# ScalarE's order in a fused attention and two-layer kernel fixed by hand: exponentials issued apart from the scores, a decode step of VectorE placed earlier, the second pair's parts split by VectorE

## The chip, the cores and the metric

The program runs on one NeuronCore of a Trainium2 chip. Five engines work side by side, each through its own list of instructions in order: TensorE (PE, matmuls and transposes; PEld is its weight loads), VectorE (DVE), ScalarE (ACT), GpSimd (POOL) and SyncE (SP), which here only issues DMA transfers. They wait for each other through semaphores. The metric is the device time of one execution in microseconds (us), the median of several.

## What is computed

Causal attention with a memory term for 4 batches and 8 heads of 576 rows and 64 columns, then two feed-forward layers on the result. Cut to what matters:

```python
scores = scale * np.matmul(q, k.transpose(0, 1, 3, 2))      # causal mask, minus the row maximum
a = np.exp(scores); a /= a.sum(-1, keepdims=True) + 1e-09
local = np.matmul(a, v)
q_p = phi(q)                       # phi(x) = x + 1 for x > 0, else exp(x)
mem_out = np.einsum('bhsd,bhde->bhse', q_p, M_prev) / (np.einsum('bhsd,bhd->bhs', q_p, z_prev)[..., None] + 1e-06)
x = g * mem_out + (1 - g) * local  # g = sigmoid(beta), one number per head
x = softplus(x @ w_in) @ w_out     # 2304 x 512, inner width 2048
return (x @ w_a * (x @ w_b)) @ w_2 # inner width 1536
```

## The kernel before, in words

Work is float32, made of products of rounded parts: a number x is split into a high part (`qh`, `kh`, `gg`, `w`) and the rest (`ql`, `kl`), and three matmuls stand for one.

The attention works on 16 units, a unit being two heads of one batch. `attention()` is a software pipeline over them: in round n (n = 0 to 16) the unit `cur` = n makes its scores for rows 256 to 575 (`score(2)`, `score(3)`, `score(4)`), `prev` = n-1 has its exponentials transposed by TensorE (`turn`, `turn_tail`, the tiles `pe`), multiplied with v (`use`, the tile `po`) and finished, and `nxt` = n+1 has its parts made (`prep_k`: `kh`, `qh`, `kl`, `ql`; `prep_v`, `prep_v2`: `pos`, `neg`, `ph`, which is phi of q) and its first two score blocks done. `score(i)` is matmuls into `ps`, an instruction of VectorE that masks, scales and takes the row minimum (`mn`), and an exponential on ScalarE (`e`; `eT` for the last 64 rows of both heads). `memory` is the memory term (`pm` in PSUM, `mo` in SBUF), `turn_memory` transposes it into `mt`, `spread` transposes the reciprocal row sums into `pr`; ScalarE copies both out (`mt`, `rb`). `turn(A, ...)` has its PSUM tile copied out by ScalarE, `turn(V, ...)` by VectorE (both into `aT`). `finish` multiplies and adds (`xx`, by VectorE and then GpSimd), and SyncE stores `xx`.

The tiles `pe`, `pm`, `mt` and `pr` share one PSUM pool, `psT`, of two banks: a transpose into a new tile waits until the tile two before it has been copied out. In each round the order on TensorE ends with `mt`, a score block, `pr`, and ten short matmuls (`pt`); the next round begins with the transposes of head 0 (copied by ScalarE, called "first `aT`" below) and head 1 (copied by VectorE), a score block, and then two more groups of four transposes that take over those two banks.

Beside the attention `beside()` brings in the first weights of the feed-forward layers: a load (`wraw`), two VectorE instructions and a ScalarE one (lines 115, 118, 120), two and one more (122, 123 and the rounding copy `w`), one VectorE subtraction. Each `yield` of `attention()` runs one such step; rounds 1 to 16 have two yields each.

The order on PE, DVE and SP within the attention is that of the code (`manual_schedule`); ScalarE's and GpSimd's is chosen by the scheduler when the program is built, from a model of its own. The bank that a tile of a pool gets is chosen then too.

Of the kernel before, what the change touches and what calls it, by code (L numbers as in the profile page):

```python
# [10 lines left out]
AF = mybir.ActivationFunctionType  # L11
ALU = mybir.AluOpType
# [3 lines left out]
NP = H // 2  # L16
# [22 lines left out]
def tile_kernel(ctx: ExitStack, tc: tile.TileContext, qt, kt, vt, mp, zp, be, w_in, w_out, w_a, w_b, w_2, out):  # L39
    nc = tc.nc  # L40
    V, A, G, PE, SP = nc.vector, nc.scalar, nc.gpsimd, nc.tensor, nc.sync

    def f(ap):
        return ap.bitcast(F32)

    def rnd(eng, o, i):

        if eng is A:
            A.activation(out=o, in_=i, func=AF.Copy)  # L49
        elif eng is V:  # L50
            V.tensor_copy(out=o, in_=i)
        else:
            G.tensor_scalar(out=o, in0=i, scalar1=1.0, scalar2=0.0, op0=ALU.mult, op1=ALU.add)

    def sub(eng, o, a, b):
        eng.tensor_tensor(out=o, in0=a, in1=b, op=ALU.subtract)  # L56
# [22 lines left out]
    for j in range(2):  # L79
        G.affine_select(  # L80
            out=mask2[64 * j : 64 * j + 64, 1, 224:], in_=mask2[64 * j : 64 * j + 64, 1, 224:], compare_op=ALU.is_ge, fill=MASKED,
# [7 lines left out]
    gp = cst.tile([128, NP], F32, name="gp")  # L89
# [5 lines left out]
    def gates():  # L95
        A.activation(out=gt, in_=bt, func=AF.Exp, scale=-1.0)
        G.tensor_scalar(out=gt, in0=gt, scalar1=1.0, scalar2=1.0, op0=ALU.mult, op1=ALU.add)
        V.reciprocal(out=gt, in_=gt)
        pairs = gt.rearrange("p (n j) -> p n j", j=2)
        for j, r in enumerate(both):  # L100
            rnd(G, gp[r], pairs[r, :, j])
        G.tensor_scalar(out=og, in0=gt, scalar1=-1.0, scalar2=1.0, op0=ALU.mult, op1=ALU.add)
# [3 lines left out]
    later = mybir.DependencyInfo(mybir.DependencyClass.NoSync, mybir.DependencyReason.SCHED_ONLY)  # L106
# [47 lines left out]
    def load_m(b):  # L154
        m = mzs[b % 2]
        for j, r in enumerate((top, low)):
            SP.dma_start(out=m[r, :, 64 * j : 64 * j + 64], in_=mp[b, r])
            SP.dma_start(out=m[r, :, 128 + j], in_=zp[b, r])
        return G.tensor_tensor(out=m[:, :, 0:128], in0=m[:, :, 0:128], in1=gp.unsqueeze(2).to_broadcast([128, NP, 128]), op=ALU.mult)

    def heads(t, n, w=64):

# [2 lines left out]
    class Unit:  # L165
# [16 lines left out]
            SP.dma_start(out=vr[:, 0:4], in_=vt[b, p, 0:512].rearrange("(c p) e -> p c e", p=128))  # L182
            SP.dma_start(out=vr[0:64, 4], in_=vt[b, p, 512:576])

        def prep_k(self, first=False, after=None, hold=None):
            kr, qr = self.kr, self.qr
            part = lambda n, w: ap_.tile([128, w], F32R, tag=n, name=n, bufs=2)
            self.qh, self.ql, self.kh, self.kl = part("qh", 640), part("ql", 640), part("kh", S), part("kl", S)
            e = V if first else G
            if hold is None:  # L190
                rnd(e, self.kh, kr)
            else:
                i0 = G.tensor_scalar(out=self.kh, in0=kr, scalar1=1.0, scalar2=0.0, op0=ALU.mult, op1=ALU.add)
                tc.add_manual_dep(i0.ins, hold.ins.name, later, reason="order")
            i1 = A.activation(out=self.qh, in_=qr, func=AF.Copy)
            if after is not None:
                tc.add_manual_dep(i1.ins, after.ins.name, later, reason="order")
            sub(e, self.kl, kr, f(self.kh))
            sub(e, self.ql, qr, f(self.qh))

# [14 lines left out]
        def score(self, i):  # L215

            if i == 0:
                self.sm, self.mn, self.E = self.small("sm"), self.small("mn"), {}
            qh, ql, kh, kl, sm, mn, Es = self.qh, self.ql, self.kh, self.kl, self.sm, self.mn, self.E

            terms = ((qh, kh), (qh, kl), (ql, kh))
            ps = psS.tile([128, 2, 512], F32, tag="b", name="ps")
            if i < 4:
                L = 128 * (i + 1)
                qc = slice(128 * i, 128 * i + 128)
                for t, (a, b) in enumerate(terms):
                    for j, r in enumerate(both):
                        PE.matmul(out=ps[:, j, :L], lhsT=a[r, qc], rhs=b[r, 0:L], start=t == 0, stop=t == 2)  # L228
                wide = i > 1
                for j in range(2):  # L230
                    n = 2 * i + j
                    e = ap_.tile([128, 512 if wide else 256], F32, tag=f"e{wide}", name="e", bufs=8)[:, :L]
                    V.tensor_tensor_reduce(  # L233
                        out=e, in0=ps[:, j, :L], in1=mask1[:, 512 - L :], scale=-0.125, scalar=BIG, op0=ALU.add, op1=ALU.min,
                        accum_out=mn[:, n : n + 1],
                    )
                    A.activation(out=e, in_=e, func=AF.Exp, scale=-1.0, bias=mn[:, n : n + 1], accum_out=sm[:, n : n + 1])  # L237
                    Es[i, j] = e
                return
            e = ap_.tile([128, S], F32, tag="eT", name="eT", bufs=2)  # L240
            for c in range(2):
                cs = slice(288 * c, 288 * c + 288)
                for t, (a, b) in enumerate(terms):
                    PE.matmul(out=ps[:, c, :288], lhsT=a[:, 512:640], rhs=b[:, cs], start=t == 0, stop=t == 2)  # L244
            V.tensor_tensor_reduce(
                out=e.rearrange("p (c n) -> p c n", c=2), in0=ps[:, :, :288], in1=mask2, scale=-0.125, scalar=BIG,
                op0=ALU.add, op1=ALU.min, accum_out=mn[:, 8:9],
            )
            A.activation(out=e, in_=e, func=AF.Exp, scale=-1.0, bias=mn[:, 8:9], accum_out=sm[:, 8:9])
            Es["t"] = e  # L250

        def memory(self):

# [174 lines left out]
    order = [Unit(b, p) for b in range(B) for p in range(NP)]  # L428

    def attention():  # L430

        nu = len(order)
        order[0].loads_k()
        A.dma_start(out=bt, in_=be.partition_broadcast(128))
        order[1].loads_k()
        order[0].loads_v()
        order[0].prep_k(True)
        order[0].score(0)
        gates()
        order[0].score(1)  # L440
        first = load_m(0)
        order[0].prep_v()
        order[0].prep_v2()
        for n in range(nu + 1):
            cur = order[n] if n < nu else None
            prev = order[n - 1] if n else None
            nxt = order[n + 1] if n + 1 < nu else None
            i1 = None
            if prev:
                i1 = prev.turn(A, [(0, 0)])  # L450
                prev.turn(V, [(1, 0)])
            if nxt:
                nxt.prep_k(after=i1, hold=None if n else first)
            if cur:
                cur.score(2)
            if prev:
                prev.turn(A, [(0, 1), (0, 3)])
                prev.turn(V, [(1, 1), (1, 3)])
            if cur:
                cur.score(3)  # L460
            if prev:
                prev.over()
            if cur:
                cur.score(4)
                cur.sums()
            if prev:
                prev.turn(A, [(0, 2), (1, 2)])
                prev.turn_tail()
            if n + 2 < nu:
                order[n + 2].loads_k()  # L470
            if nxt:
                nxt.loads_v()
                if nxt.p == 0:
                    load_m(nxt.b)
                nxt.prep_v()
                nxt.score(0)
            if cur:
                cur.memory()
            if prev:
                prev.use()  # L480
                prev.turn_memory()
                yield n
            if nxt:
                nxt.score(1)
                nxt.prep_v2()
            if prev:
                yield n
                prev.spread()
                prev.finish()


# [24 lines left out]
                yield  # L516

    steps = beside()
    with tc.manual_schedule(engines={PE.engine, V.engine, SP.engine}):
        for n in attention():  # L520
            next(steps, None)
        for _ in steps:
            pass
# [21 lines left out]
    for gi, subs in enumerate(groups):  # L545
        xbs, ys, pend = [], [], []
        for b0, nb in subs:
# [3 lines left out]
            else:  # L551
                t = [psY2.tile([128, 2, TB], F32, tag=f"z{i}", name=f"z{i}") for i in range(KT // 2)]
# [131 lines left out]
```

## Time and profile before

| | |
|---|---|
| time, median of 3 runs | 1083.64 us (1083.64 to 1083.74) |
| the profiled execution: time, span | 1083.99 us, 1082.1 us |
| busy share of the span: PE, DVE, ACT, POOL | 97%, 44%, 41%, 15% |
| mean granted clock of TensorE | 0.996 of full speed |
| attention | about the first 240 us of the span |

The span is from the first to the last instruction of the profiled execution; what lies around it is 1.9 us. The profiled execution stands 0.35 us above the median of the runs. A busy share is a mean over stages with different limits: the feed-forward layers, after 240 us, have TensorE busy nearly throughout, and the attention is where engines wait for each other.

### The profile page before, as it was taken

The page shows a single profiled execution, that of the slowest core. Times are in us where ns is not written, and L with a number is a line of the kernel's source. Part 1 is how long each engine was busy: PE and PEld are TensorE (multiplying, and loading weights), DVE is VectorE, ACT ScalarE, POOL GpSimd, SP SyncE. Part 2 cuts the span into 40 slices and gives each one's busy share as a digit, 9 for nine tenths or more (in the row PEclk, how much of TensorE's full clock was granted, in tenths as well). Part 3 has the DMA queues.
Part 4 walks back from the last instruction along what each step waited for, and adds up shares of the span by engine and source line. Part 5 has one row for each costly group of instructions (what it writes and reads, how often), then busy time and mean ns, then how long its engine had stood idle before and what let it go on. Part 6 is the DMA issues. An engine that isn't in the chain of part 4 may idle for free.

```text
span 1082.1 us, 14889 instructions
## 1 busy us (share of the span) xinstructions
PE 1054.9 (97%) x5832; PEld 863.4 (80%) x5832; DVE 477.8 (44%) x1043; ACT 448.1 (41%) x924; POOL 165.9 (15%) x178
## 2 busy tenths in 40 slices
PE   5999999999999999999999999999999999999998
PEld 4776666678888988888888888888888888888897
DVE  4778787776776211111156679742122111111121
ACT  6888877764555322232244554432112111211121
POOL 7777776521000000000000000000000000000000
PEclk9999999999999999999999999999999999999999
DMA  5143425213434200010033354421000000100010
GB/s 170 57 135 104 151 91 157 85 61 110 155 117 156 89 10 1 36 43 1 1 98 98 117 175 141 152 78 59 1 0 20 20 1 1 39 1 1 1 39 21
DMA packets 45974, 75.43 MB, mean 70 GB/s; under 512 B 9552, under 2 KB 28496, under 8 KB 45904
## 3 DMA queue, kind: packets, MB, share of 16 engines
q1 hardware_dynamic: 45616, 74.15, 21.3%
q8 instruction: 46, 0.75, 0.3%
q10 hardware_dynamic: 288, 0.33, 0.1%
q14 instruction: 24, 0.20, 0.1%
HBM read 60.31 MB, written 14.16 MB: 69 GB/s over the span
## 4 chain that ended last, share of the span: by engine, by line
PE 89%; ACT 3%; POOL 2%; DMA 2%; issue 1%; DVE 1%; SPq 0%; ACTq 0%; DVEq 0%; POOLq 0%
PE pp L142 27%; PE ph L142 18%; PE y L142 16%; PE o L142 14%; PE ps L228 2%; PE pe L299 2%; PE po L341 2%; PE z L142 2%; PE pm L262 1%; PE ps L244 1%; ACT e L237 1%; DMA qr<-qt 1%; POOL neg L56 1%; PE pe L321 1%; PE mt L350 1%
## 5 line engine op out<-in xcount | busy, mean ns | idle before, releaser
L142 PE MATMUL pp<-xb,w 128*128 128x512 f32 (+1 forms) x1440 | 305.5, 368 | 0.0
L142 PEld LDWEIGHTS pp<-xb,w 128*128 128x128 f32 x1440 | 252.5, 188 | 46.0
L142 PE MATMUL ph<-xb,w 128*128 128x512 f32 (+1 forms) x960 | 210.5, 369 | 0.0
L142 PEld LDWEIGHTS ph<-xb,w 128*128 128x128 f32 x960 | 168.1, 189 | 30.4 <-issue 0.2
L142 PE MATMUL y<-gg,w 128*128 128x512 f32 x768 | 184.3, 389 | 0.0
L142 PEld LDWEIGHTS y<-gg,w 128*128 128x128 f32 x768 | 143.9, 188 | 29.8
L621 DVE TENSOR_TENSOR u<-pp,u 128x512 f32<-128x512 f32 (+1 forms) x60 | 38.3, 638 | 271.2 <-PE pp L142 271.2
L142 PE MATMUL o<-w,gg 128*128 128x512 f32 x648 | 157.0, 390 | 0.0
L142 PEld LDWEIGHTS o<-w,gg 128*128 128x128 f32 x648 | 120.8, 188 | 24.5
L56 DVE TENSOR_TENSOR gg<-s,gg 128x512 fp32r<-128x512 f32 (+1 forms) x80 | 51.0, 637 | 176.7 <-ACT gg L49 176.5
L390 ACT ACTIVATE s<-ph 128x512 f32<-128x512 f32 (+1 forms) x80 | 44.3, 554 | 165.5 <-PE ph L142 165.4
L620 ACT ACTIVATE u<-pp 128x512 f32<-128x512 f32 (+1 forms) x60 | 33.3, 556 | 176.4 <-PE pp L142 176.3
L49 ACT ACTIVATE gg<-u 128x512 fp32r<-128x512 f32 (+1 forms) x60 | 35.2, 587 | 120.4 <-DVE u L621 120.4
L237 ACT ACTIVATE e<-e,mn 128x128 f32<-128x128 f32 (+3 forms) x128 | 70.6, 555 | 4.0 <-DVE mn L233 3.9
L233 DVE CUSTOM_DVE_ANT_0 e<-ps,mask 128x128 f32<-128x128 f32 (+3 forms) x128 | 57.6, 487 | 22.1 <-PE ps L228 18.8
L120 ACT ACTIVATE wraw<-wraw 128x512 f32<-128x512 f32 x68 | 44.9, 674 | 37.0 <-DVE wraw L118 35.4
L299 PE MATMUL pe<-ident,e 128*128 128x128 f32 x320 | 47.7, 288 | 12.3 <-ACT mt L352 8.1
L49 ACT ACTIVATE w<-wraw 128x512 fp32r<-128x512 f32 x68 | 44.7, 671 | 31.9 <-DVE wraw L123 31.9
L56 DVE TENSOR_TENSOR w<-wraw,w 128x512 fp32r<-128x512 f32 x68 | 48.0, 718 | 15.9 <-ACT w L49 15.5
L299 PEld LDWEIGHTS pe<-ident,e 128*128 128x128 f32 x320 | 36.6, 145 | 21.2 <-ACT mt L352 9.6
L56 DVE TENSOR_TENSOR gg<-u,gg 128x512 fp32r<-128x512 f32 (+1 forms) x60 | 38.3, 638 | 32.2 <-ACT gg L49 32.2
L123 DVE SCALAR_TENSOR_TENSOR wraw<-wraw 128x512 uint32<-128x512 uint32 x68 | 49.3, 737 | 1.4
(97 smaller groups left out, 1038.2 us busy)
## 6 DMA issues: line engine op xcount, KB each, us to landing
wraw<-w_in SPq DMA_DIRECT2D x16, 512.0 KB, 3.6
wraw<-w_out SPq DMA_DIRECT2D x16, 512.0 KB, 4.7
wraw<-w_a SPq DMA_DIRECT2D x12, 512.0 KB, 3.7
wraw<-w_b SPq DMA_DIRECT2D x12, 512.0 KB, 3.6
wraw<-w SPq DMA_DIRECT2D x12, 512.0 KB, 3.6
qr<-qt SPq DMA_DIRECT2D x15, 320.0 KB, 3.5
kr<-kt SPq DMA_DIRECT2D x16, 288.0 KB, 3.2
xraw<-xs SPq DMA_DIRECT2D x9, 512.0 KB, 3.9
```

The lines of the kernel that those rows point to most:

```text
L49: A.activation(out=o, in_=i, func=AF.Copy)
L56: eng.tensor_tensor(out=o, in0=a, in1=b, op=ALU.subtract)
L120: A.activation(out=f(high), in_=f(high), func=AF.Identity, scale=REBIAS)
L123: V.scalar_tensor_tensor(out=high, in0=high, scalar=3, in1=low, op0=ALU.logical_shift_left, op1=ALU.bitwise_or)
L142: mm[0] = PE.matmul(out=o, lhsT=w(a), rhs=x(b), start=start and n == 0, stop=stop and n == 2, **kw)
L228: PE.matmul(out=ps[:, j, :L], lhsT=a[r, qc], rhs=b[r, 0:L], start=t == 0, stop=t == 2)
L233: V.tensor_tensor_reduce(out=e, in0=ps[:, j, :L], in1=mask1[:, 512 - L :], scale=-0.125, scalar=BIG, op0=ALU.add, op1=ALU.min, accum_out=m ...
L237: A.activation(out=e, in_=e, func=AF.Exp, scale=-1.0, bias=mn[:, n : n + 1], accum_out=sm[:, n : n + 1])
L299: PE.transpose(out=ps[:, 128 * n : 128 * n + 128], in_=Es[i, j][:, 128 * k : 128 * k + 128], identity=ident)
L390: A.activation(out=s, in_=ph, func=AF.Softplus)
L620: A.activation(out=u, in_=pab[0], func=AF.Copy)
L621: V.tensor_tensor(out=u, in0=pab[1], in1=u, op=ALU.mult)
```

## The change

- `attention()` now runs with ScalarE's order fixed too (`A.engine` in the set of `manual_schedule`). The exponentials are no longer issued in `score`, but by a method `exps`, at places of their own: those of score blocks 0 and 1, which the scheduler had spread, stand after `rb` and after the first `aT`, and that of `eT` stands directly behind `rb`.
- `neg` of the next unit (the exponential of phi) stands behind `rb` instead of ahead of `mt`.
- The first of the two yields in a round stands after `turn_tail`, so that its VectorE instructions run before the evacuation of score block 0, where they had run after `mo`.
- The second unit's `kh`, `kl`, `ql` are made by VectorE (`prep_k(True)` in round 0), where GpSimd made them.
- `gates()` comes behind the first two exponentials; the two artificial dependencies (`after`, `hold`) are gone.

```diff
-        def prep_k(self, first=False, after=None, hold=None):
+        def prep_k(self, first=False):
...
-            if hold is None:
-                rnd(e, self.kh, kr)
-            else:
-                i0 = G.tensor_scalar(out=self.kh, in0=kr, scalar1=1.0, scalar2=0.0, op0=ALU.mult, op1=ALU.add)
-                tc.add_manual_dep(i0.ins, hold.ins.name, later, reason="order")
-            i1 = A.activation(out=self.qh, in_=qr, func=AF.Copy)
-            if after is not None:
-                tc.add_manual_dep(i1.ins, after.ins.name, later, reason="order")
+            rnd(e, self.kh, kr)
+            rnd(A, self.qh, qr)
...
-                    A.activation(out=e, in_=e, func=AF.Exp, scale=-1.0, bias=mn[:, n : n + 1], accum_out=sm[:, n : n + 1])
...
-            A.activation(out=e, in_=e, func=AF.Exp, scale=-1.0, bias=mn[:, 8:9], accum_out=sm[:, 8:9])
...
+        def exps(self, *keys):
+
+            for k in keys:
+                e, n = self.E[k], 8 if k == "t" else 2 * k[0] + k[1]
+                A.activation(out=e, in_=e, func=AF.Exp, scale=-1.0, bias=self.mn[:, n : n + 1], accum_out=self.sm[:, n : n + 1])
...
+        order[0].prep_v()
         order[0].score(0)
+        order[0].exps((0, 0), (0, 1))
         gates()
         order[0].score(1)
-        first = load_m(0)
-        order[0].prep_v()
         order[0].prep_v2()
+        load_m(0)
...
-            if nxt:
-                nxt.prep_k(after=i1, hold=None if n else first)
+            if nxt and n:
+                nxt.prep_k()
             if cur:
+                cur.exps((1, 0))
                 cur.score(2)
...
             if cur:
+                cur.exps((1, 1))
                 cur.score(3)
+            if n == 0:
+                nxt.prep_k(True)
...
             if prev:
                 prev.turn(A, [(0, 2), (1, 2)])
                 prev.turn_tail()
+            if cur:
+                cur.exps((2, 0), (2, 1))
+            if prev:
+                yield n
...
-                nxt.prep_v()
                 nxt.score(0)
             if cur:
+                cur.exps((3, 0), (3, 1))
                 cur.memory()
+            if nxt:
+                nxt.prep_v()
             if prev:
                 prev.use()
                 prev.turn_memory()
+            if nxt:
+                nxt.score(1)
+            if prev:
+                prev.spread()
+            if cur:
+                cur.exps("t")
+                cur.sums()
+            if prev:
                 yield n
             if nxt:
-                nxt.score(1)
+                nxt.exps((0, 0), (0, 1))
                 nxt.prep_v2()
             if prev:
-                yield n
-                prev.spread()
                 prev.finish()
...
-    with tc.manual_schedule(engines={PE.engine, V.engine, SP.engine}):
+    with tc.manual_schedule(engines={PE.engine, V.engine, A.engine, SP.engine}):
```

How this moves instructions is shown at three places. The first is ScalarE around the end of a round; this is a round of before, from the copy `rt` to the `qh` of the round after it (no decode step happens to stand in it).

```order
L335 ACTIVATE rt<-pt 128x192
L237 ACTIVATE e,sm<-e,mn 128x128 x2
L209 ACTIVATE neg<-neg 128x640
L352 ACTIVATE mt<-mt 128x512
L359 ACTIVATE rb<-pr 128x512
L237 ACTIVATE e,sm<-e,mn 128x256 x2
L305 ACTIVATE aT<-pe,og 128x512
L195 ACTIVATE qh<-qr 128x640
```

The same engine with the change, round 1, between the same two instructions; L120 is a decode step that stands there in some rounds.

```order
L333 ACTIVATE rt<-pt 128x192
L248 ACTIVATE e,sm<-e,mn 128x384 x2
L248 ACTIVATE e,sm<-e,mn 128x512 x2
L199 ACTIVATE pos<-qr 128x640
L350 ACTIVATE mt<-mt 128x512
L357 ACTIVATE rb<-pr 128x512
L248 ACTIVATE eT,sm<-eT,mn 128x576
L120 ACTIVATE wraw<-wraw 128x512
L248 ACTIVATE e,sm<-e,mn 128x128 x2
L203 ACTIVATE neg<-neg 128x640
L303 ACTIVATE aT<-pe,og 128x512
L49 ACTIVATE qh<-qr 128x640
```

`mt` and `rb` have `pos` and the exponentials of blocks 2 and 3 ahead of them where `neg` stood, and between `rb` and the first `aT` there are now `eT`, two exponentials of 128 columns and `neg` (and in some rounds a decode step), where two of 256 columns stood.

The second place is TensorE in a middle round, before: the second four-transpose groups of `prev` and the waits that they carry.

```order
L228 MATMUL ps<-kh,ql 128x384 x2
L299 MATMUL pe<-ident,e 128x128 [waits Activation_49]
L299 MATMUL pe<-ident,e 128x128 x3
L299 MATMUL pe<-ident,e 128x128 [waits DVE_49]
L299 MATMUL pe<-ident,e 128x128 x3
L228 MATMUL ps<-kh,qh 128x512 x2
```

The same place with the change.

```order
L222 MATMUL ps<-kh,ql 128x384 x2
L297 MATMUL pe<-ident,e 128x128 [waits DVE_49]
L297 MATMUL pe<-ident,e 128x128 x3
L297 MATMUL pe<-ident,e 128x128 [waits Activation_49]
L297 MATMUL pe<-ident,e 128x128 x3
L222 MATMUL ps<-kh,qh 128x512 x2
```

TensorE's order is the same, but the two groups have exchanged banks: the first now waits for VectorE's `aT` and the second for ScalarE's. This is so in 13 of the 14 rounds from 2 to 15; round 8 is as before.

The third place is ScalarE at the end of the attention, the last round but one, before.

```order
L352 ACTIVATE mt<-mt 128x512
L359 ACTIVATE rb<-pr 128x512
L120 ACTIVATE wraw<-wraw 128x512
L390 ACTIVATE s<-ph_3512 128x512
L305 ACTIVATE aT<-pe,og 128x512
```

With the change (`s` is the softplus of the first feed-forward layer, which has another function table than the exponential).

```order
L350 ACTIVATE mt<-mt 128x512
L357 ACTIVATE rb<-pr 128x512
L248 ACT_TABLE_LOAD
L248 ACTIVATE eT,sm<-eT,mn 128x576
L120 ACTIVATE wraw<-wraw 128x512
L388 ACT_TABLE_LOAD
L388 ACTIVATE s<-ph_3512 128x512
L303 ACTIVATE aT<-pe,og 128x512
```

The last unit's `eT` now stands behind the first two softplus instructions, and two more table loads stand around it. On the other engines: VectorE has the three instructions of the second unit's parts and the moved decode steps; GpSimd makes `ph` after `xx` and `neg` ahead of `ss`; on SP the loads of the first decode step and two loads of `xraw` come ahead of the `kr` and `qr` loads that they had followed.

## Rows read from the trace of the kernel before

**Rows 1.** Busy time by stretch: length, then PE, PEld, DVE, ACT, POOL, clock, DMA.

```profile
26.00:240.00 214.00, 203.11 (x1721) 147.80 (x1718) 165.86 (x487) 166.54 (x432) 140.88 (x143) 0.98 0.34 105
```

**Rows 2.** Waits, 0 to 280 us: total, how often, the longest.

```profile
PE pe L299 <- ACT mt L352: 8.1, 9, 1.7
```

**Rows 3.** Timeline of PE: start, length, instruction, idle before it and its releaser.

```profile
34.16 0.66 PE L358 MATMUL pr<-ident,R 128*128 128x128 f32 x4
...
47.03 0.66 PE L358 MATMUL pr<-ident,R 128*128 128x128 f32 x4
...
160.88 1.15 PE L299 MATMUL pe<-ident,e 128*128 128x128 f32 x8 [1.66 <-ACT mt L352]
...
217.14 0.66 PE L358 MATMUL pr<-ident,R 128*128 128x128 f32 x4
...
220.35 1.09 PE L299 MATMUL pe<-ident,e 128*128 128x128 f32 x8
```

**Rows 4.** Groups of ACT, 26 to 240 us: count, busy, mean ns, idle before.

```profile
L305 ACT ACTIVATE aT<-pe,og 128x512 f32<-128x512 f32 x30 | 20.4, 680 | 1.9 <-PE pe L299 1.3
...
L249 ACT ACTIVATE eT<-eT,mn 128x576 f32<-128x576 f32 x15 | 11.5, 769 | 0.0
L237 ACT ACTIVATE e<-e,mn 128x128 f32<-128x128 f32 x28 | 10.9, 392 | 0.0
L209 ACT ACTIVATE neg<-neg 128x640 f32<-128x640 f32 x13 | 9.6, 737 | 24.0 <-POOL neg L56 24.0
...
L120 ACT ACTIVATE wraw<-wraw 128x512 f32<-128x512 f32 x10 | 6.8, 681 | 0.7 <-DVE wraw L118 0.7
...
L390 ACT ACTIVATE s<-ph 128x512 f32<-128x512 f32 x3 | 1.8, 599 | 5.8 <-PE ph L142 5.8
```

**Rows 5.** Timeline of ACT after `pr` in round 14.

```profile
217.89 0.60 ACT L359 ACTIVATE rb<-pr 128x512 f32<-128x512 f32 x1 [0.50 <-PE pr L358]
218.39 0.49 ACT L237 ACTIVATE e<-e,mn 128x256 f32<-128x256 f32 x1
```

**Rows 6.** Timelines of DVE and POOL: a decode instruction beside GpSimd and alone.

```profile
171.74 1.69 DVE L122 TENSOR_SCALAR wraw<-wraw 128x512 f32<-128x512 f32 x1
...
171.60 1.54 POOL L56 TENSOR_TENSOR neg<-qr,pos 128x640 f32<-128x640 f32 x1
...
217.94 0.43 DVE L122 TENSOR_SCALAR wraw<-wraw 128x512 f32<-128x512 f32 x1
```

**Rows 7.** Timelines of PE and DVE in the first 26 us.

```profile
17.18 0.47 PE L228 MATMUL ps<-kl,qh 64*128 64x128 f32 x2 [2.39 <-POOL kl L56]
...
24.94 0.66 PE L299 MATMUL pe<-ident,e 128*128 128x128 f32 x4 [0.59 <-ACT aT L305]
...
6.48 0.82 DVE L56 TENSOR_TENSOR ql<-qr,qh 128x640 fp32r<-128x640 f32 x1
...
12.11 0.69 DVE L233 CUSTOM_DVE_ANT_0 e<-ps,mask 128x512 f32<-128x512 f32 x1
```

**Rows 8.** Timelines of ACT and PE at the end of the attention.

```profile
226.39 1.28 ACT L390 ACT_TABLE_LOAD   x1
227.69 0.60 ACT L390 ACTIVATE s<-ph 128x512 f32<-128x512 f32 x1
...
236.31 0.59 ACT L359 ACTIVATE rb<-pr 128x512 f32<-128x512 f32 x1
...
239.20 0.68 ACT L305 ACTIVATE aT<-pe,og 128x512 f32<-128x512 f32 x1
...
239.94 1.45 PE L299 MATMUL pe<-ident,e 128*128 128x128 f32 x8 [0.39 <-ACT aT L305]
...
242.93 0.66 PE L321 MATMUL pe<-ident,eT 128*128 128x128 f32 x4 [0.66 <-DVE aT L307]
```

**Rows 9.** Busy time by stretch, columns as in rows 1.

```profile
116.00:122.00 6.00, 4.70 (x52) 3.35 (x48) 4.50 (x12) 5.18 (x11) 5.39 (x6) 1.00 0.02 5
160.00:166.00 6.00, 5.12 (x28) 3.79 (x28) 3.86 (x9) 5.69 (x14) 4.98 (x5) 0.72 0.12 37
```

More of the change, by code (lines that the diff above doesn't have):

```diff
@@ L158, in load_m @@
             SP.dma_start(out=m[r, :, 128 + j], in_=zp[b, r])
-        return G.tensor_tensor(out=m[:, :, 0:128], in0=m[:, :, 0:128], in1=gp.unsqueeze(2).to_broadcast([128, NP, 128]), op=ALU.mult)
+        G.tensor_tensor(out=m[:, :, 0:128], in0=m[:, :, 0:128], in1=gp.unsqueeze(2).to_broadcast([128, NP, 128]), op=ALU.mult)
     def heads(t, n, w=64):
@@ L447, in attention @@
             nxt = order[n + 1] if n + 1 < nu else None
-            i1 = None
             if prev:
-                i1 = prev.turn(A, [(0, 0)])
+                prev.turn(A, [(0, 0)])
                 prev.turn(V, [(1, 0)])
-            if nxt:
-                nxt.prep_k(after=i1, hold=None if n else first)
+            if nxt and n:
+                nxt.prep_k()
             if cur:
+                cur.exps((1, 0))
                 cur.score(2)
@@ L464, in attention @@
                 cur.score(4)
-                cur.sums()
             if prev:
```

## The prediction

> **What bounds the kernel now.** I read the busy time by stretch first, to see which engine has the least slack in the stage that the change touches. From 26 to 240 us TensorE is busy 203 of 214 us, VectorE 166, ScalarE 167, GpSimd 141 [rows 1]. TensorE is the bound, and whatever this change does must come through the 11 us in which it waits there, or through its granted clock (0.98 in the mean).
>
> The waits come next. The largest one that the change can reach is TensorE's second four-transpose groups waiting for ScalarE's copy `mt`: 8.1 us in nine places, 1.7 the longest [rows 2]. Why is that copy late? In ScalarE's groups `neg` has 24.0 us of idle time ahead of it, all ended by GpSimd's subtraction, in 13 rounds [rows 4]. ScalarE runs in order, and `mt` and `rb` stand behind `neg`. So the chain is: GpSimd late, ScalarE held at `neg`, the bank of `mt` not free, TensorE held.
>
> The timeline of TensorE gives the price. From one `pr` to the next an unstalled round takes 47.03 − 34.16 = 12.87 us; from the first of these to `pr` at 217.14 thirteen rounds take 182.98, or 14.08 each [rows 3]. So 1.2 us a round are lost, to idle time and to falls of the clock. The two go together in one place: after the stall of 1.66 us at 160.88 [rows 3] the stretch of 6 us shows a granted clock of 0.72, whereas the stretch from 116 to 122, with TensorE busy only 4.70 of its 6 us, shows 1.00 [rows 9].
>
> **Part 1: `neg` off the path, and what stands there instead.** With `neg` behind `rb`, neither `mt` nor `rb` waits for GpSimd, and the nine waits of [rows 2] should go. But the banks have changed hands. In 13 of 14 rounds the second of the later transpose groups now waits for ScalarE's first `aT`, and this copy has more ahead of it. I add up that chain from `pr`, by round 14 [rows 3, 5] and the means of ScalarE's groups [rows 4]:
>
> - `rb` starts 217.89 − 217.14 = 0.75 after `pr`, and the next instruction 0.50 later: 1.25.
> - `eT` 0.77 and two exponentials of 128 columns at 0.39: 2.80.
> - `neg` 0.74, of which 0.10 overlaps with its successor, as `rb` shows (0.60 long, the next one after 0.50): 3.44.
> - the first `aT` 0.68, and 0.06 until TensorE starts on it (239.20 + 0.68 against 239.94 [rows 8]): 4.18.
>
> Unstalled, the eight transposes begin 220.35 − 217.14 = 3.21 after `pr`, and the second four half of 1.09 later: 3.75. So TensorE waits 0.43 us, and such a round takes 13.30. Where a decode step of ScalarE stands in the chain (0.68 − 0.10 = 0.58), the wait is 1.01 and the round takes 13.88. Of the thirteen rounds seven have such a step, five have none, and in one, where the banks are as before, the first four wait: 4.18 − 3.21 = 0.97, or 13.84. The sum is 7 × 13.88 + 5 × 13.30 + 13.84 = 177.5, against 182.98: **−5.5**. Into the round after that the old order had no wait at 220.35 [rows 3], and the new one has 1.01: +1.0. **Net −4.5.** The chain is a sum of means. If each step were 0.2 shorter in all, this would be −7; if GpSimd's subtraction still came last, at 2.8 after `pr`, a part of the old wait would be back, and the bound there is no gain.
>
> **Part 2: the first yield after `turn_tail`.** The decode instructions of VectorE now run while GpSimd makes `kh`, `R` and `kl`. Beside a GpSimd instruction the same VectorE instruction took 1.69 us, and alone 0.43 [rows 6]: a wait of 1.26. They stand ahead of the evacuation of block 0, so a late VectorE delays the scores and `mt`, which has some 0.7 us to spare now that `neg` no longer leads it. One such wait hides there; two cost about 1.2. Five rounds have two instructions in that place, and I take a wait too many in one of five, and so five times 0.25: **+1.3**, between 0 (all hidden) and 6 (two waits each time).
> The Trainium skill ("SBUF — State Buffer", section "SBUF: two separate sides") says that VectorE and GpSimd hold their shared port as an exclusive lock, for the whole of an instruction. The 1.69 against 0.43 agrees; by that page alone every moved instruction would wait, the term would be +6, and the whole about 1084.9.
>
> **Part 3: the second unit's parts by VectorE.** TensorE's largest wait in the first 26 us is 2.39, for GpSimd's `kl` at 17.18 [rows 7]. It goes when VectorE makes `kh`, `kl` and `ql`. VectorE can begin once the mask of block 3 is done, 12.11 + 0.69 = 12.80, later by some 0.8 since the reciprocal of `gates()` now waits for an exponential that stands behind two of 0.39. Three instructions of at most 0.82 (`ql` [rows 7]) take 2.0 to 2.5, and up to 1.6 more where GpSimd holds them up once (1.54 [rows 6]). The `kl` is then ready between 15.3 and 17.0, against 17.18: a gain of 0.2 to 1.9. A second wait, 0.59 for ScalarE at 24.94 [rows 7], and one of 0.2 behind it, should also go, since there is less in front of that `aT`. Together 1.0 to 2.7; I take the middle, **−1.9**.
>
> **Part 4: two table loads at the end.** The last unit's `eT` stands between softplus instructions. Before, `aT` began 239.20 − 236.31 = 2.89 after `rb` [rows 8]. Now what lies between is 0.50 for `rb`, 1.30 for a table load (226.39 to 227.69 [rows 8]), 0.77 for `eT`, 0.58 for the decode step, 1.30 for the load back and 0.50 for `s` (0.60 less the overlap): 4.95, or 2.1 later. TensorE waits for this `aT` already (0.39 at 239.94), so nothing covers it in front; but behind it TensorE waited 0.66 for VectorE's copy [rows 8], which comes in the meantime. I take **+1.7**, between 0.9 (the 0.66 and one more such wait filled) and 2.4.
> The Trainium skill ("ScalarE: Activation LUTs", section "What ACT_TABLE_LOAD costs") adds to the load of 1.28 us a drain of 1.38, 2.66 a switch; by it the end would cost 2.8 more, and the total would be 1083.0. The trace has the load at 1.28 and the next instruction 1.30 after its start [rows 8], with no room for a drain behind it; what lies ahead of it no row separates.
>
> **At nothing.** TensorE's order and the PSUM tiles' sizes are the same. SP's earlier `wraw` and `xraw` loads go past `kr` and `qr` loads that are needed a round (13 us) later, so a load that is late by one or two us is covered; without that cover each would cost its delay once. GpSimd's `ph` and `neg` change places with instructions that are needed later in the round; the `ql` at the end of its list then comes some 0.4 us before its score block. That cover is the thinnest here: with it gone TensorE would wait in each round for what is missing.
>
> **The sum.** −4.5 + 1.3 − 1.9 + 1.7 = −3.4. From the profiled execution's own 1083.99 that is 1080.6. The median of the runs is 0.35 lower, so 1080.2. About 0.2% (2.2 us) can be told from no change: faster is below 1081.5, slower above 1085.8.
>
> **Rivals.**
> *No change, 1082 to 1085.* The stall only moves from `mt` to `aT`. For it: the chain of 4.18 is already longer than TensorE's 3.75, so ScalarE gates each round, and each 0.2 us more in it costs 2.6 over thirteen rounds. Or the VectorE waits of part 2 come twice a round: −4.5 + 6 − 1.9 + 1.7 = +1.3, 1084.9. Against it: all of ScalarE's durations are measured, and its idle time at `neg` (24.0) is what it gains. The drain of the page would also end here; the row behind the load speaks against it. Chance 0.21, of which the drain has 0.03.
> *Slower through the clock, about 1087.* The new order has a stall of about 1.0 us in eight rounds, where the old one had long stalls in fewer. The stretch after a stall of 1.66 us lost (1 − 0.72) × 6 = 1.7 us [rows 9]. If stalls of 1.0 bring that too, four more falls cost 6.8, and 1080.2 becomes 1087.0; the point from which it decides is two falls for no change, four for slower. For it: the fall and the stall stand together at 160.88. Against it: 1.30 us idle in the stretch from 116 to 122 left the clock at 1.00. Chance 0.19.
> *All terms at their best.* The chain shorter by 0.2 (−2.6), part 2 hidden (−1.3), part 3 at −2.7 (−0.8), part 4 at 0.9 (−0.8): 1074.7. Each alone is likely enough, all together not; it lies with the forecast on the side of faster.
>
> **How the numbers follow.** The forecast and what is better than it: 0.60. No change: 0.21. Slower: 0.19. The likeliest is 1080.2. The range reaches down to 1075.5, short of all terms at their best, and up to 1086.5, which takes in the bound of part 2 and three to four falls of the clock; some 2 in 10 lie outside.
>
> **What the profile after would show.** Right: the waits of `pe` for `mt` gone; waits of `pe` for ScalarE's `aT` instead, 0.4 in rounds without a decode step of ScalarE and 1.0 with one; no idle time of ScalarE at `neg`; `pr` to `pr` 13.3 and 13.9; no wait of over 2 us before 26 us; two more table loads near 237 us, and the last `aT` 2.1 us later after `rb`. Wrong: stretches with a clock of 0.7 in more than two rounds; waits of TensorE for VectorE's evacuation of blocks 0 and 1 or for GpSimd's `ql`; or `neg` still waiting for GpSimd after `rb`, with `aT` late behind it.

## The result, and the profile after

The changed kernel takes 1088.55 us (median of 4 runs, 1087.59 to 1090.82), the kernel before 1083.64; the ratio of the means is 1.0051, with a 95% interval of 1.0033 to 1.0068. It is slower by half a per cent, where the prediction had 1080.2, a range up to 1086.5, and a chance of 0.19 for slower. The profiled execution after took 1088.51 us, with a span of 1086.7 (before 1082.1).

Where the 4.6 us come from is read by cutting both spans at the same instructions: the first `pr`, the fourteenth and the last. Busy time by stretch, columns as in rows 1; the first two rows are of the kernel before, whose first `pr` and fourteenth are in [rows 3].

```profile
34.16:217.14 182.98, 172.48 (x1484) 124.74 (x1483) 144.86 (x428) 144.76 (x380) 129.13 (x129) 0.98 0.38 115
217.14:246.95 29.81, 28.39 (x215) 20.98 (x214) 20.28 (x48) 17.65 (x38) 6.09 (x9) 1.00 0.16 56
```

The same two stretches of the kernel after:

```profile
30.84:215.38 184.54, 170.87 (x1484) 122.57 (x1483) 138.40 (x428) 147.77 (x382) 128.11 (x132) 1.00 0.37 114
215.38:251.57 36.19, 31.74 (x215) 22.25 (x213) 20.38 (x48) 22.37 (x47) 8.42 (x12) 0.91 0.14 46
```

TensorE does the same matmuls in both (1484 and 215). Up to the first `pr` the new order is 3.32 us ahead. The thirteen rounds take 1.56 longer: TensorE idles 13.67 us in place of 10.50, and is busy 1.61 less at a clock of 1.00 in place of 0.98. The last two rounds take 6.38 longer: 3.03 more idle, and 3.35 more busy, at 0.91 in place of 1.00. Sum: −3.32 + 1.56 + 6.38 = 4.62. Behind the last `pr` the two spans agree (835.1 us each).

TensorE's waits, 30 to 225 us, after (columns as in rows 2):

```profile
PE pe L297 <- ACT aT L303: 6.0, 9, 0.8
PE mt L348 <- DVE mo L268: 5.6, 2, 2.9
PE pe L297 <- DVE aT L305: 1.8, 6, 0.4
```

The wait for `mt` of [rows 2] is gone, and the wait for ScalarE's `aT` stands in its place, as forecast. But there is a line that the prediction does not have: twice TensorE waits for VectorE's `mo`, 5.6 us together. Timelines of ScalarE, VectorE, GpSimd and TensorE at the first of the two, in round 7:

```profile
109.90 0.60 ACT L248 ACTIVATE e<-e,mn 128x384 f32<-128x384 f32 x1
...
110.49 1.04 ACT L49 ACTIVATE xb<-xraw 128x1024 fp32r<-128x1024 f32 x1
...
111.55 1.42 POOL L56 TENSOR_TENSOR kl<-kr,kh 128x576 fp32r<-128x576 f32 x1
111.57 2.48 DVE L56 TENSOR_TENSOR xb<-xraw,xb 128x1024 fp32r<-128x1024 f32 x1 [2.62 <-ACT xb L49]
...
113.97 0.28 DVE L227 CUSTOM_DVE_ANT_0 e<-ps,mask 128x128 f32<-128x128 f32 x1
...
115.60 0.63 PE L348 MATMUL mt<-ident,mo 128*128 128x128 f32 x4 [2.94 <-DVE mo L268]
```

The moved yield brings an `xb` step in rounds 7 and 10: a rounding copy by ScalarE, then a subtraction by VectorE. ScalarE's half stands behind two exponentials in its new fixed order; VectorE's half waits 2.62 us for it, runs 2.48 us with GpSimd's `kl` beside it, and behind it, in VectorE's order, now stand the masks of block 0 and `mo`, which TensorE waits for.

The end, TensorE and ScalarE, and the clock behind it:

```profile
236.20 0.59 ACT L357 ACTIVATE rb<-pr 128x512 f32<-128x512 f32 x1
...
236.81 1.28 ACT L248 ACT_TABLE_LOAD   x1
...
238.10 0.78 ACT L248 ACTIVATE eT<-eT,mn 128x576 f32<-128x576 f32 x1
...
239.53 1.28 ACT L388 ACT_TABLE_LOAD   x1
...
241.32 0.68 ACT L303 ACTIVATE aT<-pe,og 128x512 f32<-128x512 f32 x1
...
242.06 1.09 PE L297 MATMUL pe<-ident,e 128*128 128x128 f32 x8 [2.85 <-ACT aT L303]
...
246.61 4.54 PE L339 MATMUL po<-aT,vr 128*64 128x512 f32 x16
```

```profile
245.00:249.00 4.00, 4.00 (x16) 1.65 (x16) 1.12 (x3) 0.62 (x2) 0.62 (x1) 0.50 0.00 0
```

`aT` starts 5.12 us after `rb` (4.95 forecast), TensorE waits 2.85 us for it, and then works at the lower of its two clock levels (0.50, or 1.2 GHz): its sixteen `po` matmuls take 4.54 us.

### The profile page after: what moved, and what is told of

It reads as the page before. It is cut to its first block, busy times and chain, and to the rows that moved or that the text cites. A ratio compares the mean times of both kernels' runs of the same rounds, so it can differ in the third digit from the quotient of the medians.

```text
span 1086.7 us, 14873 instructions
## 1 busy us (share of the span) xinstructions
PE 1056.4 (97%) x5832; PEld 862.8 (79%) x5832; DVE 473.4 (44%) x1046; ACT 452.5 (42%) x926; POOL 159.7 (15%) x175
## 4 chain that ended last, share of the span: by engine, by line
PE 90%; ACT 5%; DVE 3%; issue 1%; DMA 0%; ACTq 0%; POOL 0%; DVEq 0%
PE pp L142 27%; PE ph L142 18%; PE y L142 16%; PE o L142 14%; PE po L339 3%; PE ps L222 3%; PE z L142 2%; PE pm L260 2%; PE pe L297 2%; ACT e L248 1%; PE ps L237 1%; DVE e L227 1%; PE mt L348 1%; ACT neg L203 1%; ACT aT L303 1%; ACT eT L248 1%
## 5 line engine op out<-in xcount | busy, mean ns | idle before, releaser
L120 ACT ACTIVATE wraw<-wraw 128x512 f32<-128x512 f32 x68 | 45.0, 673 | 37.5 <-DVE wraw L118 35.6
L49 ACT ACTIVATE gg<-s 128x512 fp32r<-128x512 f32 (+1 forms) x80 | 47.0, 587 | 2.0
```

Source lines behind the costliest of these rows:

```text
L120: A.activation(out=f(high), in_=f(high), func=AF.Identity, scale=REBIAS)
```

## The experiments

The theory after this reading: the loss is the two waits for `mo` (xb steps), the wait at the end with the fall of the clock behind it, and the chain to the first `aT` that takes back what moving `neg` gave. Rivals: VectorE beside GpSimd in all moved steps; a clock that falls anyway; costs that only change places. Ratios are to the kernel before, run on the same chip; they are not quotients of the medians and can differ from these by 0.1%. The changed kernel's own ratio is 1.0051, and 1.0044 when run again; differences "by the ratios" are given against both.

**All first yields behind `mo`** (ahead of `pos` on ScalarE).

```diff
             if cur:
                 cur.exps((2, 0), (2, 1))
-            if prev:
-                yield n
...
                 cur.memory()
+            if prev:
+                yield n
```

> The changed kernel, with the first yield of each round moved behind the two mo multiplications of VectorE again, as before; all else as changed. Theory (an xb subtraction of VectorE waits 2.6 us for ScalarE's xb in rounds 7 and 10 and holds back mo): the two waits of TensorE for mo, 2.94 and 2.64, go and nothing else does; 5.6 us less than the changed kernel's 1088.6, about 1083.0, level with before. Rival (every moved decode instruction of VectorE is held up beside GpSimd, as part 2 of the prediction had it): more than that comes back, several us more than with the xb steps alone moved back. Second rival (the waits for mo only covered other waits): less than 2 us comes back.

Measured: 1094.96 us, ratio 1.0099 (1.0078 to 1.0121). The waits for `mo` go, yet it is slower than the changed kernel: the theory and the first rival fail, and of the second only the number holds (less than 2 us came back), not its reason. In six rounds the first of the later transpose groups waits 1.2 for VectorE's `aT`. Its timelines in round 2, GpSimd, VectorE, TensorE:

```profile
45.98 1.55 POOL L56 TENSOR_TENSOR neg<-qr,pos 128x640 f32<-128x640 f32 x1 [3.22 <-ACT pos L199]
...
46.32 1.50 DVE L122 TENSOR_SCALAR wraw<-wraw 128x512 f32<-128x512 f32 x1
...
49.99 0.66 PE L297 MATMUL pe<-ident,e 128*128 128x128 f32 x4 [1.20 <-DVE aT L305]
```

ScalarE's decode step now delays `pos`, so that GpSimd's `neg` comes late and lies beside the second yield's VectorE instruction, which takes 1.50 us. The theory of this became a run of its own.

**The same, behind `pos` on ScalarE.**

```diff
             if nxt:
                 nxt.prep_v()
             if prev:
+                yield n
                 prev.use()
```

> The changed kernel, with the first yield of every round behind mo on VectorE, as in the run that was 1.0099 of before, but behind pos on ScalarE where that run had it ahead of pos. Theory (that run lost because the decode step delayed pos, and with it GpSimd's neg, which then ran beside the decode instruction of the second yield: 1.50 us in place of 0.43, and VectorE's aT came 1.2 late): GpSimd's neg starts where it does in the changed kernel, the waits of pe for VectorE's aT go from 1.2 to 0.3, and the time comes to 1083 to 1085. Rival (VectorE's decode instructions behind mo are late by themselves): the waits of 1.2 stay and so does the time, about 1094.

Measured: 1084.01, ratio 0.9992 (0.9981 to 1.0003). Of the waits of 1.2 none is left (one of 1.58 stands behind the xb step of round 10). The order of one ScalarE instruction and `pos` was worth some 12 us by the ratios, and 8.4 between the two profiled executions. Of these, 7.8 lie in the thirteen rounds: 5.2 are idle time of TensorE and 2.6 busy time at a lower clock (0.97 against 0.99).

```profile
45.01 1.56 POOL L56 TENSOR_TENSOR neg<-qr,pos 128x640 f32<-128x640 f32 x1 [1.54 <-ACT pos L199]
...
46.85 0.42 DVE L122 TENSOR_SCALAR wraw<-wraw 128x512 f32<-128x512 f32 x1
```

**Only the xb steps behind `mo`.**

```diff
-            if prev:
+            if prev and n not in (7, 10):
                 yield n
...
                 cur.memory()
+            if n in (7, 10):
+                yield n
```

> The changed kernel, with the first yield moved behind mo in rounds 7 and 10 alone, the two in which it brings an xb step; the other twelve stay behind turn_tail. Theory (only the xb steps cost): the same as with all of them moved, within 1 us, about 1083. Rival (the other decode steps cost too, beside GpSimd): between that and the changed kernel, 2 us or more above the run with all moved.

Measured: 1083.72, ratio 0.9997 (0.9985 to 1.0009), 5 to 6 less than the changed kernel by the ratios, the waits for `mo` gone. Moving the yields of rounds 7 and 10 back gives as much as moving all of them (0.9992, the run above): where the `wraw` steps stand, behind `turn_tail` or behind `pos`, makes no difference that these intervals show. Ahead of `pos` they are dear, as the first run showed.

**The xb step ahead of the two exponentials.**

```diff
+            if prev and n in (7, 10):
+                yield n
             if cur:
                 cur.exps((2, 0), (2, 1))
-            if prev:
+            if prev and n not in (7, 10):
                 yield n
```

> The changed kernel, with the yield of rounds 7 and 10 ahead of the two exponentials of block 2 and not behind them: ScalarE's xb comes 1.2 us earlier, VectorE's order stays as changed. Theory (VectorE is held because it waits in order for ScalarE's xb, which stands behind these exponentials): VectorE's wait for xb goes from 2.6 to about 1.4, TensorE's waits for mo shrink by as much each, 2 to 2.5 us less in all. Rival (the length of the subtraction, 2.2 to 2.5 us beside GpSimd, is the whole cost): the waits for mo stay at 1.7 to 2.9, the time at the changed kernel's.

Measured: 1083.94, ratio 0.9995 (0.9985 to 1.0005); some 5 to 6 less than the changed kernel by the ratios, twice what was expected. The wait for ScalarE is 1.2 shorter, and the subtraction takes 1.23 us in place of 2.48, though GpSimd works beside it here too. The timelines of round 7, VectorE, GpSimd, TensorE:

```profile
111.90 1.23 DVE L56 TENSOR_TENSOR xb<-xraw,xb 128x1024 fp32r<-128x1024 f32 x1 [1.42 <-ACT xb L49]
...
111.98 1.68 POOL L53 TENSOR_SCALAR kh<-kr 128x576 fp32r<-128x576 f32 x1 [2.13 <-PE pm L260]
...
114.69 0.63 PE L348 MATMUL mt<-ident,mo 128*128 128x128 f32 x4 [0.50 <-DVE mo L268]
```

The same `kh` in round 7 of the changed kernel, where no subtraction stood beside it:

```profile
110.79 0.67 POOL L53 TENSOR_SCALAR kh<-kr 128x576 fp32r<-128x576 f32 x1 [2.47 <-DMA kr<-kt]
```

What differs is who starts first. In the changed kernel GpSimd's `kl` starts at 111.55 and VectorE's subtraction 0.02 later, and VectorE's is the long one; here VectorE starts 0.08 ahead, and GpSimd's `kh` takes 1.68 in place of 0.67. So both theory and rival hold a part: in round 7, 1.2 us of the wait for `mo` is ScalarE's order, and 1.25 (2.48 less 1.23) is GpSimd ahead of VectorE. That lock is the one of the Trainium skill ("SBUF — State Buffer", section "SBUF: two separate sides"); the trace agrees, with 2.48 and 2.18 where GpSimd had started first, against 1.23 and 1.31 where VectorE had.

**The last `eT` ahead of the softplus.**

```diff
                 cur.exps((3, 0), (3, 1))
+                if n == nu - 1:
+                    cur.exps("t")
...
-                cur.exps("t")
+                if n < nu - 1:
+                    cur.exps("t")
```

> The changed kernel, with the last unit's eT issued behind its other exponentials, ahead of the softplus instructions: two table loads fewer. Theory (the wait of TensorE of 2.85 us at 242 us comes from the loads, and the fall of the clock to 0.58 and 0.85 in the 12 us around it from that wait): the wait shrinks to about 0.4, the granted clock from 240 to 252 is 1.00, and pr to pr in the last round goes from 16.1 to 11.3: 4.7 us less, about 1083.9. Rival (the clock falls there for another reason): the wait goes, the clock falls all the same, 2.1 less, about 1086.4.

Measured: 1085.81, ratio 1.0004 (0.9989 to 1.0018), 4 to 5 less than the changed kernel by the ratios, as the theory had it. The last `pr` to `pr` is 12.27 in place of 16.07, at a clock of 1.00. It is not 11.3, since the wait of 2.85 becomes 0.95 and not 0.4, and waits of 0.30 and 1.05 for VectorE's `aT` stand behind it:

```profile
239.16 0.66 PE L297 MATMUL pe<-ident,e 128*128 128x128 f32 x4 [0.95 <-ACT aT L303]
...
242.31 0.66 PE L319 MATMUL pe<-ident,eT 128*128 128x128 f32 x4 [1.05 <-DVE aT L305]
```

**The first `aT` ahead of the exponentials and `neg`.**

```diff
                 prev.turn(V, [(1, 0)])
-            if nxt and n:
-                nxt.prep_k()
+                if cur:
+                    cur.exps((0, 0), (0, 1))
+                    cur.prep_v2()
             if cur:
-                cur.exps((1, 0))
                 cur.score(2)
...
                 prev.turn(V, [(1, 1), (1, 3)])
+            if nxt and n:
+                nxt.prep_k()
             if cur:
-                cur.exps((1, 1))
+                cur.exps((1, 0), (1, 1))
...
-            if nxt:
-                nxt.exps((0, 0), (0, 1))
-                nxt.prep_v2()
```

> The changed kernel, with the first aT put ahead of the two exponentials of 128 columns and of neg on ScalarE, the second aT ahead of qh and of the two exponentials of 256 columns. Theory (the chain rb, eT, decode step, two exponentials, neg, first aT is what TensorE waits for, 0.6 and 0.3 in a round): the chain is 1.4 us shorter, the waits of pe for aT go to below 0.2, rounds without xb take 12.9 to 13.2 in place of 13.35 and 14.0, 7 to 9 us less in all, about 1080. Rival (neg, qh and with them GpSimd's ph and ql come later, and TensorE waits for these): waits of the score blocks for ql or of pm for ph appear, and less than 3 us is gained.

Measured: 1082.57, ratio 0.9979 (0.9965 to 0.9992), some 7 to 8 less than the changed kernel by the ratios. TensorE's waits, 30 to 225 us:

```profile
PE mt L348 <- DVE mo L268: 3.4, 2, 1.7
PE pr L356 <- POOL R L284: 2.3, 1, 2.3
PE pe L297 <- ACT aT L303: 2.1, 6, 1.1
PE pe L297 <- DVE aT L305: 0.3, 1, 0.3
```

Of 6.0 and 1.8 for `aT` 2.1 and 0.3 remain, and eight of the thirteen rounds take 12.9 to 13.3. The waits for `mo` are 2.2 shorter too, and a new one of 2.3 for GpSimd's `R` takes that back. The rival's waits, for `ql` or `ph`, do not show in this stretch.

**`neg` ahead of `mt` again.**

```diff
             if nxt:
                 nxt.prep_v()
+                nxt.prep_v2()
...
                 nxt.exps((0, 0), (0, 1))
-                nxt.prep_v2()
```

> The changed kernel, with neg of the next unit ahead of mt and rb on ScalarE, as before. Theory (in the order of before, ScalarE waits for GpSimd's subtraction and mt comes late; moving neg removed this): waits of pe for mt of about 1 us come back in most rounds, rb and the first aT come later by as much, rounds of 14 to 15 us, 6 to 13 us slower than the changed kernel. Rival (the place of neg is of no account, since the chain to aT is only longer behind rb and shorter ahead of it): within 2 us of the changed kernel.

Measured: 1098.3, ratio 1.0135 (1.012 to 1.015), ten above the changed kernel. The old wait is back, and the wait for `aT` stays (30 to 240 us):

```profile
PE pe L297 <- ACT mt L350: 11.6, 13, 1.5
PE pe L297 <- ACT aT L303: 5.8, 9, 1.7
```

**The second unit's parts by GpSimd.**

```diff
             if n == 0:
-                nxt.prep_k(True)
+                nxt.prep_k()
```

> The changed kernel, with the second unit's kh, kl and ql made by GpSimd as before. Theory (these are what TensorE waits for at 14 to 18 us): the waits for GpSimd's kh and kl of 1 and 2.4 us come back, the first pr stands at 33.5 to 34.2 in place of 30.8, 3 us slower, about 1091. Rival (the rest of the new order at the start brings the gain): the first pr moves by less than 1 us.

Measured: 1087.27, ratio 1.0037 (1.0022 to 1.0051), and the first `pr` at 30.21, no later than with VectorE: the theory fell. GpSimd makes `kh` at 6.47 us there, since nothing holds it. What held it before was the dependency on the first scaled `mz`, so this was put back.

**GpSimd, and held as before.**

```diff
+                i0 = G.tensor_scalar(out=self.kh, in0=kr, scalar1=1.0, scalar2=0.0, op0=ALU.mult, op1=ALU.add)
+                tc.add_manual_dep(i0.ins, hold.ins.name, later, reason="order")
...
-        load_m(0)
+        held = load_m(0)
...
-                nxt.prep_k(True)
+                nxt.prep_k(hold=held)
```

> The changed kernel, with the second unit's parts made by GpSimd and its kh held until the first mz is scaled, as before (the run that had them made by GpSimd did not hold it). Theory (at the start the gain comes from dropping this hold, whichever engine makes the parts): TensorE waits 2 us or more for GpSimd's kl at about 16 us, the first pr comes 2 to 3 us later than the 30.2 of that run, 2 to 3 us slower than it, about 1089.5 to 1090.5. Rival (the gain comes from ScalarE's and GpSimd's order in the first round): the first pr within 1 us of 30.2.

Measured: 1090.42, ratio 1.0051 (1.0034 to 1.0069). The wait of [rows 7] is back, and the first `pr` comes at 32.08, 1.9 later than without the hold. The intervals of the two ratios overlap, so the time does not tell them apart, but the wait does:

```profile
16.62 0.33 PE L226 MATMUL ps<-kl,qh 64*128 64x128 f32 x2 [2.54 <-POOL kl L56]
```

**The changed kernel again.**

> The changed kernel itself once more. Theory: two waits of TensorE for mo of 1.7 to 2.9 us, a wait of 2.85 for the last aT; if the fall of the clock follows that last wait, the granted clock falls again below 0.7 in the 8 us behind it, as it did in five of the seven profiles that have this wait. Time 1.003 to 1.007 of before. Rival for the clock (chance): it stays at 1.00 there.

Measured: 1088.36, ratio 1.0044 (1.0028 to 1.006); waits for `mo` of 2.80 and 2.62, for the last `aT` 2.85, and a granted clock of 0.66 in the stretch behind it. (Of the seven profiles that the expectation counts six, and not five, show this fall.) The waits are those of the first profile, but the clock lies elsewhere. The thirteen rounds and the last two:

```profile
31.49:218.23 186.74, 174.83 (x1484) 125.84 (x1482) 139.16 (x428) 147.77 (x382) 128.11 (x132) 0.97 0.37 113
218.23:252.03 33.80, 29.96 (x214) 22.13 (x213) 20.40 (x48) 22.36 (x47) 8.44 (x12) 0.95 0.16 49
```

Against the kernel before, the thirteen rounds take 3.76 longer here (1.41 idle, 2.35 busy) and the last two 3.99 (2.42 idle, 1.57 busy); the first `pr` is 2.67 ahead. In the rounds the clock falls twice, behind the two waits for `mo` (0.50 from 116 to 120, 0.57 from 163 to 167), and stands at 1.00 behind all the shorter waits for `aT`.

**Three edits together**, and the same with GpSimd making the second unit's parts.

> The changed kernel with three edits together: the xb steps of rounds 7 and 10 behind mo, the last eT ahead of the softplus instructions, and the first aT ahead of the two exponentials and neg. Theory (the three costs are separate): against the kernel of before, 2 us less by the first aT alone, 3.5 more by the waits for mo gone, 3 to 4 more by the end: 8 to 10 us faster than before, 1074 to 1076 where before is 1084. Rival (one cost hides behind another, or falls of the clock take the gain): 2 to 5 us faster than before.

> The three edits that together were 0.991 of before, and the second unit's parts made by GpSimd without a hold. Theory (the engine that makes these parts is of no account): the same ratio within 0.002. Rival (VectorE's part of the change is worth 1 us or more): 0.993 or above.

Measured: 1074.4, ratio 0.991 (0.9895 to 0.9925), and 1072.19, ratio 0.989 (0.9869 to 0.9911). One by one the three edits gave 5 to 6, 4 to 5 and 7 to 8 us by the ratios, 16 to 19 in all; together they give 14 to 18. So the costs are separate, or nearly so. Both are faster than the kernel before and the changed one; which engine makes the second unit's parts cannot be told. The thirteen rounds of the last one, from first to fourteenth `pr`:

```profile
31.20:203.22 172.02, 168.97 (x1484) 122.89 (x1482) 140.13 (x428) 147.79 (x382) 127.03 (x132) 1.00 0.39 122
```

Against 182.98 and 184.54, they are within 5 us of thirteen unstalled rounds (13 × 12.87 = 167.3).

## Why the prediction was wrong, point by point

**The bound and the old stall: right.** TensorE's waits for `mt` came from `neg`; they went with the change and came back with `neg` ahead of `mt`.

**Part 1, the chain to `aT`: right, with little gained.** The forecast was 13.30 for a round without a decode step of ScalarE, 13.88 with one, 13.84 for the round with the banks as before. Outside the two xb rounds the trace has 13.33 to 13.36, 13.91 to 14.15, and 13.78. Without the two waits for `mo` (5.58) the thirteen rounds take 178.96, against a forecast of 177.5 before part 2: an excess of 1.5. In most rounds with a decode step the wait of about 1.0 comes in two parts, some 0.3 for VectorE's `aT` and 0.65 for ScalarE's; the first was not foreseen. Running `aT` first showed that this chain is what they wait for.

**Part 2: the step that failed.** "Five rounds have two instructions in that place, and I take a wait too many in one of five": the count took in the `wraw` steps alone. Those cost nothing measurable, and the +6 at which every moved instruction would wait did not come. The two xb steps, which the same yield brings, were not looked at: VectorE's half waits in order for ScalarE's, which the change had put behind two exponentials, and then finds GpSimd ahead of it. The term was +1.3; the two waits are 5.58 (2.94 and 2.64), and moving these two steps alone gave 5 to 6 us back. The bound of 6 was near by luck: it stood for another mechanism (two locks in each of five rounds).

**Part 3: right in sign, the mechanism too narrow.** The gain was 3.32 up to the first `pr` (2.67 in the second profile), of which 0.62 is an earlier first matmul (5.70 against 6.32), and 2.7 the rest; the forecast was 1.9. The wait of 2.39 for `kl` went, as forecast, but VectorE is not needed for that: GpSimd without the hold does without the wait too, and with the hold it is back (2.54). How much of the gain in time the hold is worth stays open. With it the first `pr` was still 2.08 ahead of the kernel before, and the 1.9 between the runs with and without it contain a fall of the clock too (0.50 from 17 to 19.5 us in the run with it).

**Part 4: the idle time right, the price behind it missed.** `aT` 2.1 us later after `rb` was forecast, and 2.2 measured. The last two rounds idle 3.03 more, against 1.0 + 1.7 forecast. What was not in the sum is the clock: 3.35 us in this execution, 1.57 in the second profile, which has 2.35 more busy time in the rounds instead. The rival with the clock, which came nearest in time, had it fall in the eight rounds with stalls of 1.0. There it fell in neither profile; it fell behind the one wait of 2.85 and, in the second profile, behind the two for `mo`. Taking the table loads out cut the wait to 0.95, and the fall was gone. The drain that the Trainium skill ("ScalarE: Activation LUTs", section "What ACT_TABLE_LOAD costs") adds to a load is not in this trace on either side: `rb` ends at 236.79, the load starts at 236.81 and `eT` at 238.10.

By terms: forecast −3.4, measured +4.6. The 8.0 us between them are part 2 and the small excess of the rounds (+5.8), the end (+3.7, nearly all of it clock), and the start (−1.4).

## What to carry to other kernels

When a step is moved that is shared by two engines, follow the second engine's half to the first engine's half, in each kind of step that the place can bring, and not only in the commonest. When an engine's order is written out, look for what stands ahead of each instruction that a bound engine waits for, and put that copy first: here one copy put ahead of three instructions, two steps moved and one exponential moved earlier turned 0.5% slower into 1% faster. Where the clock falls behind a wait, the wait costs more than its length, and it is worth removing even where it stands alone.

## What the runs showed of the hardware that was not expected

The fall of the clock is neither sure nor set by the length of one wait alone. Of ten profiles with the 2.85 us wait at the end (the changed kernel twice and eight of the variants), nine show a granted clock of 0.50 to 0.67 in a stretch of 4 us behind it (a part or all of it at the lower level, 1.2 GHz), and one (the first `aT` ahead) shows 1.00 throughout; the four profiles without that wait (before, the last `eT` moved, both combinations) show 1.00. In the kernel before, the clock was 0.72 in the 6 us around each of two waits of 1.66 and 1.65; in the run with all first yields behind `mo`, 0.50 from 52 to 56 us, behind waits of 1.20 and 0.63 close to each other. At the wait for `mo` of round 7 the same kernel did both. In the first profile of the changed kernel, after a wait of 2.94, the stretch behind it has 1.00:

```profile
116.00:120.00 4.00, 3.99 (x47) 2.91 (x44) 2.80 (x8) 3.13 (x9) 1.46 (x3) 1.00 0.02 4
```

In its second profile, after a wait of 2.80, it has 0.50:

```profile
116.00:120.00 4.00, 3.97 (x30) 3.08 (x30) 1.76 (x7) 1.40 (x3) 0.86 (x1) 0.50 0.01 4
```

What decides between these stayed open. It means that on average the two waits for `mo` may cost more than their 5.6 us of idle time.

In the first 13 to 25 us the matmuls take up to twice as long as later while the column of the granted clock says 1.00. When this ends differs by run. (In the run with only the xb steps behind `mo` it ends before 16 us, and a second slow stretch follows, which the column does show: 0.50 from 17.5 to 21 us.) With the three edits, eight transposes at 19.83 take

```profile
19.83 1.94 PE L297 MATMUL pe<-ident,e 128*128 128x128 f32 x8 [0.25 <-DVE mo L268]
```

and in the changed kernel 1.06 at 19.48:

```profile
19.48 1.06 PE L297 MATMUL pe<-ident,e 128*128 128x128 f32 x8 [0.33 <-DVE mo L268]
```

The first `pr` of the run with the three edits is at 33.80, where the same start in other runs gave 30.8 to 32.4. So a shift of the first `pr` by 2 us between two kernels can be this alone, and what is said of part 3 rests on its waits more than on its times. Why the column shows 1.00 there stayed open.
